# A spectral and windowed-attention mixer on one core: another layout of the spectra, and another order of early transfers

## The chip, the core and the metric

The program runs on one core of a Trainium2 chip. The metric is the device time of one execution in microseconds. TensorE is written PE, its weight loads PEld, VectorE DVE, ScalarE ACT, GpSimd POOL, and SyncE, which here only issues transfers, SP. ACT issues transfers too.

## The reference

The input is x, 2048 rows of 640 numbers in float32. Two branches are computed from it and mixed by a gate per row.

```python
g = _sigmoid((x * gate_w).sum(-1, keepdims=True))
a = _A_ref(x, A_wqkv, A_wo)      # q, k, v = x @ wqkv; 32 heads of 20; each row attends to 8 rows, 2 apart; @ wo
b = _B_ref(x, B_w_r, B_w_i)      # irfft2(rfft2(x) * (w_r + 1j * w_i))
return g * a + (1 - g) * b
```

## The kernel before

**Rows.** The 2048 rows are split as 128 partitions by 16 positions j (row = 16 p + j). A transform over rows is then a transform over the 128 partitions (a product with a table of cosines and sines) and one over the 16 positions.

**Recording and planning.** No instruction is issued where it is written. `Plan.record` (L224) notes every operation with what it must follow, `Plan.order` (L282) searches an order for each of the five engines with made-up costs, and `issue` (L472) then issues them in that order. That is why nearly all instructions of the profile carry the same line, L655: parts are told apart by the names of their tiles. An engine works through its list strictly in order, so an instruction that waits holds up everything behind it on that engine, transfers that it would issue included. `p.chain` and `p.rank` are hints for the search.

**Stages.** They overlap, and the PE list runs through them in this order:

1. `qkv` (L719): eight units (par, hg), each eight groups of 15 products of 480 columns. ACT copies a PSUM bank to `ev`, and for each pair ACT issues a store to `qkvd` in device memory. The weights of the next hg come by `load_w` (L673): SP loads `raw{hg}_{t}`, ACT makes a rounded copy and POOL the rest.
2. `attend` (L759): 16 halves of units, each a chain over DVE, POOL and ACT. Keys `kt` come by SP, queries `q` and values `vt` by ACT (L774 to L776), all from `qkvd`. ACT copies two positions of q at a time to `qbank`, DVE multiplies into `pr` and sums into the logits `L`. `mask` (L826) lets ACT write -1e9 to a few places of one partition of L. Units 0 and 4 come first.
3. `fold` and `cols` (L840, L878): x folded by symmetry, then products with the table `fc` into z; ACT copies z to `zg`, the spectra. `fold` of q = 2 and 3 stores its result to `fd` in device memory (L872) for later.
4. `freq` (L900): 16 groups g of frequencies, four staged at a time. A group takes its 8 columns (4 frequencies, real and imaginary) of the 16 positions: 128 numbers per chunk t. Weight of a product are these 128 columns, and the moving operand a table `bt`. This gives u and v, DVE makes ab = u + vv and u - vv, then come a transform over positions (xa, xc), the product with the filter (POOL, DVE: P, p, s), and the way back (g), which ACT copies to `zg`.
5. `project_even` (L1110), in between: rows j even of the attention output times wo (oTp, woa, wob).
6. `spatial` (L1025): for each position j, products whose weights are the 128 columns of `zg` at that j, and whose moving operand is the table `gt`: oa and ob, each one product of 322 columns and two of 161. Then ha and hb.
7. `project_odd` (L1126): rows j odd, to the end.

A float32 product is two passes on PE, each with its own weight load; the page counts passes, so oa has 16 x 3 x 2 = 96.

**What the change touches in `freq` and `spatial`.** `zg` lies as (chunk t, position j, 128 columns): the 128 columns at one t and j, the weights of `spatial`, are side by side. Those of a group are 16 runs of 8. So `freq` first copies them to `zc`, with the halves of the complex numbers exchanged in three further chunks for v:

```python
zc = self.zcr.next(f"zc{g}", 6, NJ, 8)
A.copy(zc[:, 0:3], zg[:, 0:3, :, 8 * g : 8 * g + 8])
A.mul(zc[:, 3:6, :, 0:4], zg[:, 2:5, :, 8 * g + 4 : 8 * g + 8], -1.0)
A.copy(zc[:, 3:6, :, 4:8], zg[:, 2:5, :, 8 * g : 8 * g + 4])
```

Of the kernel before, what the change touches and what calls it, by code (L numbers as in the profile page):

```python
# [17 lines left out]
NJ = 16  # L18
# [14 lines left out]
def dft_tables():  # L33
# [23 lines left out]
    bt = np.zeros((640, 642))  # L57
# [8 lines left out]
    j, k2 = np.arange(16), np.arange(16)  # L66
    md = np.zeros((16, 16, 2, 4, 2, 16, 4))
# [40 lines left out]
        first[x, x, 0] = g0  # L108
        first[x, x, 1, :, :, :, 0], first[x, x, 1, :, :, :, 1] = -g0[:, :, :, 1], g0[:, :, :, 0]
    first[:, :, :, :, :, 0, :, :, 0] = one  # L110
    first = first.reshape(8, 128, 128).transpose(1, 0, 2).reshape(128, 1024)
    mfu, mfv = mf[0].copy(), mf[0].copy()
    for q, w in ((mfu, mu), (mfv, mv)):
        q[:, :, 0] = 0
        q[:, :, 0, :, :, 0] = w
    first = np.concatenate([first, mfu.reshape(128, 128), mfv.reshape(128, 128)], 1)
    md = md.reshape(16, 128, 2, 64)
    mm = np.concatenate([-md[:, :, 1], md[:, :, 0], md[:, :, 1], mf.reshape(16, 128, 128)], 2)[1:]

    d = np.arange(161)  # L120
# [20 lines left out]


class Op:
    __slots__ = ("i", "eng", "name", "call", "busy", "lat", "size", "preds", "succs", "chain", "tail", "start", "end", "early", "group", "of", "two", "rank")


class Engine:
# [9 lines left out]
class Plan:  # L157
# [5 lines left out]
    def __init__(self, nc):  # L163
        self.ops, self.places, self.past = [], {}, set()
        self.chain = self.group = ""
        self.rank = 0.0
        self.code = {}
        for attr, eng, real in (
            ("pe", "PE", nc.tensor),
            ("dve", "DVE", nc.vector),  # L170
            ("act", "ACT", nc.scalar),
            ("pool", "POOL", nc.gpsimd),
            ("sp", "SP", nc.sync),
        ):
            setattr(self, attr, Engine(self, eng, real))
# [48 lines left out]
    def record(self, eng, name, fn, a, k):  # L224
        op = Op()
        op.i, op.eng, op.name, op.chain, op.group = len(self.ops), eng, name, self.chain, self.group
        op.preds, op.succs, op.size, op.early, op.two, op.rank = set(), [], 0, False, False, 0.0
        line = sys._getframe(2).f_lineno
        code = self.code.get(line)
        if code is None:  # L230
            code = self.code[line] = compile("\n" * (line - 1) + "fn(*a, **k)", __file__, "exec")
        op.call = (code, {"fn": fn, "a": a, "k": k})
        aps = [v for v in list(a) + list(k.values()) if hasattr(v, "tensor") and hasattr(v, "ap")]
        out = k["out"] if "out" in k else a[0]
        ins = [v for v in aps if v is not out]
        for v in ins:
            self.touch(op, v, False)
        self.touch(op, out, True)
        op.of = out.tensor.name
        self.cost(op, out, ins, k)  # L240
        self.ops.append(op)

    def cost(self, op, out, ins, k):
        n = max(int(np.prod(v.shape[1:])) for v in [out] + ins[:1])
        if op.name == "dma_start":
            op.busy, op.lat = {"SP": 0.45, "ACT": 0.45, "POOL": 1.0}[op.eng], LAND
            op.size = int(np.prod(out.shape)) * 4
            op.early = not hasattr(ins[0].tensor, "tag")
            if self.rank:
                op.rank, self.rank = self.rank, self.rank - 1e3  # L250
        elif op.eng == "PE":
            n = int(np.prod(out.shape[1:]))
            if op.name == "transpose":
                op.busy = 0.109
            elif ins[-1].dtype == F32R:
                op.busy = n / 2400 + 0.018
            else:
                op.busy = max(4 * n / 2400 + 0.006, 0.182)
            op.lat = 0.25
        elif op.eng == "DVE":  # L260
            op.busy, op.lat = 0.075 + n / 960, 0.12
            two = sum(v.tensor.tag[:4] not in ("bank", "qban") for v in ins) == 2
            if op.name == "scalar_tensor_tensor":
                op.busy += 0.06
            elif op.name == "reciprocal":
                op.busy += n * 0.007
            elif two:
                op.two = True
        elif op.eng == "ACT":
            strided = any(len(v.ap) > 2 and v.ap[-1][0] > 1 for v in [out] + ins)  # L270
            op.busy, op.lat = 0.12 + n * (1.75e-3 if strided else 0.78e-3), 0.15
            if len(ins) > 1:
                op.busy += 0.1
            if any(v.offset >= 64 * v.ap[0][0] for v in [out] + ins):
                op.busy += 0.08
        else:
            spread = any(v.ap[-1][0] == 0 for v in ins)
            op.busy, op.lat = 0.09 + n * (2e-3 if spread else 2.25e-3), 0.14
        if op.eng in ("DVE", "ACT", "POOL") and not op.size:
            op.busy *= PACE  # L280

    def order(self):  # L282
# [7 lines left out]
        for op in reversed(ops):  # L290
            op.tail = max([s.tail + self.lag(op, s) for s in op.succs], default=0.0)
            if op.size:
                op.tail += op.size / RATE
            key = (op.eng, op.chain)
            if key in last and (op.eng == "PE" or op.chain and op.eng != "ACT"):
                op.tail = max(op.tail, last[key].tail)
            op.tail += op.busy
            last[key] = op
        span = max(op.tail for op in ops)
        for op in ops:  # L300
            op.early = max(FOLD * (op.chain == "fold"), span - op.tail - AHEAD) if op.early and not op.rank else 0.0
# [211 lines left out]
class Mixer:  # L513
# [17 lines left out]
    def places(self, pp, dr, sb):  # L531
# [15 lines left out]
        def ring(*tags):  # L547
            return Ring(sb, *tags)

        def n(tag, k):  # L550
            return ring(*(f"{tag}{i}" for i in range(k)))
# [5 lines left out]
        self.xr, self.wr, self.evr, self.rawr, self.fr = n("x", 8), ring(*WPLACES), n("ev", 2), n("raw", 5), n("f", 2)  # L557
        self.er, self.xor = ring("fe0", "fe1"), ring("raw0", "raw1", "raw2", "raw3", "raw4", "kv4", "kv5", "ya")

        self.zcr, self.vsr, self.mdr, self.mfr, self.wpr = n("raw", 2), ring("raw2"), n("ev", 2), ring("mf"), n("f", 2)  # L560
        self.abr, self.Pr, self.s12r, self.Xr = ring("x0", "x1"), ring("x2", "x3"), ring("x4", "x5"), ring("raw3", "raw4")
        self.p1r = ring("x6")

        self.wor, self.war, self.yar = ring("ya", "w7"), ring("w2", "w3", "w4", "w0", "w1", "w5", "w6"), ring("ya")
        self.otr, self.oTr = (ring("w7"), ring("w7", "kv2")), (ring("x7"), ring("x7", "pr0"))
# [12 lines left out]
    def work(self):  # L578
# [26 lines left out]
        for hg in (1, 2, 3):  # L605
            self.load_w(None, hg)
            self.qkv(0, hg)
            if hg == 1:
                self.qkv(1, hg)
        self.zg = self.one("zg", 5, NJ, 128, tag="big")  # L610
        todo = list(range(8))

        def columns(jj):
# [59 lines left out]
    def load_w(self, st, hg):  # L673
# [4 lines left out]
        for t in range(5):  # L678
# [2 lines left out]
            hi.append(w[:, 0, 0:n])  # L681
            lo.append(w[:, 1, 0:n])
            if st is None:
                p.sp.dma_start(raw, src[t])
            p.chain = "w" if st is None else ""
            p.act.copy(hi[t], raw)
            (p.dve if st is not None else p.pool).tensor_sub(lo[t], raw, hi[t].bitcast(F32))
# [71 lines left out]
    def attend(self, par, h, step=4):  # L759
# [11 lines left out]
        p.chain = "logits"  # L771
        kt, vt = (self.kvr.next(f"{i}t{nm}", 15, HC) for i in "kv")
        q = self.qr.next(f"q{nm}", 8, HC)
        self.queue("kt").dma_start(kt.rearrange("p a b -> p (a b)"), rows(1, 0, 15), max_dma_last_dim=PACKET)  # L774
        self.queue("q").dma_start(q.rearrange("p a b -> p (a b)"), rows(0, 7, 8), max_dma_last_dim=PACKET)
        self.queue("vt").dma_start(vt.rearrange("p a b -> p (a b)"), rows(2, 0, 15), max_dma_last_dim=PACKET)  # L776
        L = self.Lr.next(f"L{nm}", 8, 4, 8)
        for jj in range(0, 8, 2):
            pr = self.prr.next(f"pr{nm}{jj}", 2, 8, HC)
# [60 lines left out]
    def fold(self, q):  # L840
# [28 lines left out]
        V.tensor_sub(f[:, :, 161:321], e[:, :, 0:160], eh[:, :, 160:0:-1])  # L869
        self.folded[q] = f  # L870
        if q in STORED:
            p.act.dma_start(self.f_d[:, q], f)  # L872

    def load_f(self, q):
        f = self.folded[q] = self.fr.next(f"f{q}", 2, 641)[:, :, 0:640]
# [2 lines left out]
    def cols(self, q):  # L878
        p = self.p
        f = self.folded[q]  # L880
        for t0, n in ((0, 2), (2, 2), (4, 1)):
            z = self.ps(BQ, f"z{q}_{t0}")
            for i in range(2 * n):
# [8 lines left out]
                )  # L892
            p.chain = "z"
            p.act.copy(
                self.zg[:, t0 : t0 + n, 2 * q : 2 * q + 2, :].rearrange("p t j c -> p t (j c)"),
                z[:, 0 : 256 * n].rearrange("p (t m) -> p t m", t=n),
            )
            p.chain = ""

    def freq(self, g):  # L900
# [12 lines left out]
        wp = self.wpr.next(f"wp{g}", 4, 321)  # L913
        self.queue("wp").dma_start(wp, ins["ws"][g])

        zc = self.zcr.next(f"zc{g}", 6, NJ, 8)
        A.copy(zc[:, 0:3], zg[:, 0:3, :, 8 * g : 8 * g + 8])
        A.mul(zc[:, 3:6, :, 0:4], zg[:, 2:5, :, 8 * g + 4 : 8 * g + 8], -1.0)
        A.copy(zc[:, 3:6, :, 4:8], zg[:, 2:5, :, 8 * g : 8 * g + 4])

        def row(o, t, r, start, stop):
            T.matmul(o, zc[:, t].rearrange("p j c -> p (j c)"), r, start=start, stop=stop, skip_group_check=True)

        v = self.ps(BV, f"v{g}")[:, 0:321]
        row(v, 4, bt[:, 803:1124], True, False)
        row(v[:, 0:161], 3, bt[:, 642:803], False, False)
        row(v[:, 161:321], 5, bt[:, 1124:1284], False, True)
        vv = self.vsr.next(f"vs{g}", 321)
        A.copy(vv, v)
        u = self.ps(BU, f"u{g}")[:, 0:321]  # L930
        row(u, 1, bt[:, 161:482], True, False)
        row(u[:, 0:161], 0, bt[:, 0:161], False, False)
# [7 lines left out]
        def col(nm, i, turned):  # L940
# [7 lines left out]
                c = 0 if turned else 64  # L948
                T.matmul(o, tb[:, c : c + 128], ab[:, i], start=True, stop=True)
            return o  # L950

        def turn(to, o):

            A.mul(to[0:64], o[64:128], -1.0)
            A.copy(to[64:128], o[0:64])

        X = self.Xr.next(f"X{g}", 2, 321)
        o = col("xa", 0, 0)
# [32 lines left out]
        for t0, n in ((0, 3), (3, 2)):  # L991
            o = self.ps(BG, f"g{g}_{t0}")
            for i in range(n):
# [8 lines left out]
                        skip_group_check=True,  # L1002
                    )
            A.copy(
                zg[:, t0 : t0 + n, :, 8 * g : 8 * g + 8],
                o[:, 0 : n * 128].rearrange("p (t j c) -> p t j c", t=n, c=8),
            )

    def load_wo(self):
# [15 lines left out]
    def spatial(self, j):  # L1025
# [3 lines left out]
        o1, o2 = (self.ps((0, 1, 2), f"o{i}{j}") for i in "ab")  # L1029

        def mm(o, t, r, start, stop):
            T.matmul(o, zg[:, t, j], r, start=start, stop=stop, skip_group_check=True)

        mm(o1[:, 0:322], 1, gt[:, 161:483], True, False)
        mm(o1[:, 0:161], 0, gt[:, 0:161], False, False)
# [201 lines left out]
```

## Time and profile before

| | |
|---|---|
| time, median of 3 runs | 453.15 us (453.03 to 455.2) |
| the profiled execution's own time | 452.6 us |
| its span | 450.8 us |
| PE busy | 443.1 us, 2437 products |
| DVE busy | 393.0 us |
| POOL busy | 339.3 us |
| ACT busy | 217.8 us, 578 instructions |
| transfers | 98.65 MB, 219 GB/s on average |
| granted PE clock | 1.00 |

Instruction spans on PE overlap: a product's span is longer than its distance to the next. The distance is read from the chain of work that ended last, where consecutive pieces are laid end to end, or from the start of the next row. "Idle before" is the time in which an engine had nothing running, with what ended it.

### The profile page before, as it was taken

How to read it: one execution, taken by the hardware profiler on the slowest of the kernel's cores; microseconds unless marked ns; L12 is line 12 of the kernel's file. 1: busy time of each engine (PE TensorE's matmuls, PEld its weight loads, DVE VectorE, ACT ScalarE, POOL GpSimd, SP SyncE). 2: the span in 40 equal slices, each digit the busy share in tenths (PEclk: the TensorE clock that was granted, in tenths of full speed). 3: DMA queues.
4: the chain of work that ended last, by engine and by line, in shares of the span. 5: the costliest groups of instructions: out<-in, count | busy, mean ns of one | idle time of the engine just before them, and what ended most of it. 6: DMA issues, size and time to landing. Idle time of an engine off the chain costs nothing. (4 is left out here: it accounts for less than half of the span.)

```text
span 450.8 us, 7124 instructions
## 1 busy us (share of the span) xinstructions
PE 443.1 (98%) x2437; PEld 388.8 (86%) x2437; DVE 393.0 (87%) x515; ACT 217.8 (48%) x578; POOL 339.3 (75%) x296
## 2 busy tenths in 40 slices
PE   9999999999999999999999999999999999999996
PEld 5888888888888889888987887899888999999996
DVE  5465699999999999999999999999999999989442
ACT  6464264324332333444558787878664654342120
POOL 1085047789999998899559899936498977967895
PEclk9999999999999999999999999999999999999999
DMA  8998949685665839999798676867634231769842
GB/s 313 371 316 283 354 148 313 209 273 138 210 195 160 247 115 284 300 288 288 230 268 294 177 246 191 282 222 239 197 120 129 86 98 52 190 170 230 295 147 87
DMA packets 87283, 98.65 MB, mean 219 GB/s; under 512 B 20416, under 2 KB 74816, under 8 KB 87248
## 3 DMA queue, kind: packets, MB, share of 16 engines
q1 hardware_dynamic: 47616, 63.64, 44.6%
q10 hardware_dynamic: 38864, 32.86, 23.7%
q0 software_dynamic: 768, 1.71, 2.1%
q8 instruction: 19, 0.31, 0.3%
q14 instruction: 16, 0.13, 0.1%
HBM read 66.33 MB, written 30.22 MB: 214 GB/s over the span
## 5 line engine op out<-in xcount | busy, mean ns | idle before, releaser
L655 PE MATMUL qkv<-w,xo 128*128 128x480 f32 (+1 forms) x480 | 114.2, 386 | 0.0
L655 PE MATMUL qkv<-w,xe 128*128 128x480 f32 (+1 forms) x465 | 105.3, 383 | 0.0
L655 PEld LDWEIGHTS qkv<-w,xo 128*128 128x128 f32 x480 | 89.2, 189 | 13.3 <-ACT ev L655 0.2
L655 PEld LDWEIGHTS qkv<-w,xe 128*128 128x128 f32 x465 | 87.4, 188 | 15.1 <-POOL w L655 0.5
L655 ACT COPY ev<-qkv 128x480 f32<-128x480 f32 x64 | 35.6, 558 | 46.6 <-PE qkv L655 29.6
L655 PE MATMUL woa<-wo,oT 128*128 128x320 f32 x240 | 47.7, 315 | 0.3 <-ACT oT L655 0.3
L655 PE MATMUL wob<-wo,oT 128*128 128x320 f32 x240 | 47.9, 317 | 0.0
L655 PEld LDWEIGHTS woa<-wo,oT 128*128 128x128 f32 x240 | 38.0, 188 | 0.8 <-ACT oT L655 0.6
L655 PEld LDWEIGHTS wob<-wo,oT 128*128 128x128 f32 x240 | 38.1, 188 | 0.4
L655 POOL TENSOR_TENSOR P<-X,wp 128x642 f32<-128x642 f32 x16 | 25.1, 1566 | 14.9 <-ACT X L655 14.7
L655 POOL TENSOR_TENSOR w<-raw,w 128x480 fp32r<-128x480 f32 x15 | 18.0, 1239 | 19.8 <-ACT w L655 19.8
L655 POOL TENSOR_TENSOR xo<-xt,xo 128x640 fp32r<-128x640 f32 x8 | 12.4, 1573 | 21.9 <-ACT xo L655 21.9
L655 ACT CAST oT<-oTp 128x384 fp32r<-128x384 f32 (+1 forms) x32 | 13.2, 428 | 28.6 <-PE woa L655 12.0
L655 PEld LDWEIGHTS g<-mm,s 128*128 128x128 f32 x150 | 21.9, 191 | 5.3 <-issue 0.7
L655 PE MATMUL g<-mm,s 128*128 128x128 f32 x150 | 23.5, 276 | 1.0 <-DVE s L655 0.8
L655 DVE TENSOR_TENSOR oT<-oTp,oT 128x384 fp32r<-128x384 f32 (+1 forms) x32 | 15.1, 484 | 8.9 <-ACT oT L655 8.9
L655 PE MATMUL oa<-gt,zg 128*128 128x161 f32 (+1 forms) x96 | 22.8, 344 | 0.0
L655 PE MATMUL ob<-gt,zg 128*128 128x161 f32 (+1 forms) x96 | 22.7, 345 | 0.0
L655 PE MATMUL v<-bt,zc 128*128 128x321 f32 (+2 forms) x96 | 22.2, 345 | 0.4 <-ACT zc L655 0.4
L655 PE MATMUL u<-bt,zc 128*128 128x321 f32 (+2 forms) x96 | 22.1, 344 | 0.0
L655 PEld LDWEIGHTS u<-bt,zc 128*128 128x128 f32 x96 | 15.8, 190 | 2.9
L655 PEld LDWEIGHTS v<-bt,zc 128*128 128x128 f32 x96 | 15.6, 190 | 3.0 <-ACT zc L655 0.6
(305 smaller groups left out, 1091.4 us busy)
## 6 DMA issues: line engine op xcount, KB each, us to landing
qkvd<-ev ACTq DMA_DIRECT2D x32, 480.0 KB, 4.1
wp<-in_ws SPq DMA_DIRECT2D x16, 642.0 KB, 4.6
fx<-in_x SPq DMA_DIRECT2D x8, 648.0 KB, 7.3
ot<-od SPq DMA_DIRECT2D x16, 320.0 KB, 3.8
raw<-in_wqkv SPq DMA_DIRECT2D x15, 240.0 KB, 5.0
xt<-in_xT SPq DMA_DIRECT2D x8, 320.0 KB, 8.6
ad<-ya SPq DMA_DIRECT2D x8, 320.0 KB, 2.5
yi<-ad SPq DMA_DIRECT2D x8, 320.0 KB, 3.8
```

Source lines behind the costliest of these rows:

```text
L655: p.dve.memset(w, 0.0)
```

## The change

`zg` now lies as (t, group g, the 8 columns c of the group, position j). The 128 numbers of a group at one t are side by side and are the weights of u and v directly; `zc` is gone. The tables are permuted to fit (columns outside, positions inside). The exchange of the halves for v is made on v itself, when ACT copies it from PSUM: two copies of 64 partitions (`turn`) for one of 128. The copy of z to `zg` now writes numbers 16 apart (64 bytes), and the copy of g to `zg` writes whole runs. In `spatial` the 128 weights of a position are 16 numbers, or 64 bytes, apart. The place of `zc` goes to a second buffer of `vs` and of p.

Second, a flag `hold` on some transfers: in the plan they follow the first key and query loads (unit 0, half a). They are the weights of hg = 2, the keys and queries of half b of unit 0, the values of half a, and the stores of `fold`. The planner is told so; no wait is added on the chip by it, only the lists change.

```diff
@@ dft_tables
-    first = first.reshape(8, 128, 128).transpose(1, 0, 2).reshape(128, 1024)
+    first = first.transpose(0, 1, 2, 4, 5, 3, 6, 7, 8).reshape(8, 128, 128).transpose(1, 0, 2).reshape(128, 1024)
...
-    md = md.reshape(16, 128, 2, 64)
+    md = md.transpose(0, 2, 3, 1, 4, 5, 6).reshape(16, 128, 2, 64)
+    mf = mf.transpose(0, 1, 2, 3, 5, 6, 4)
@@ Plan.order
+        for op in ops:
+            if op.hold:
+                op.preds.update(self.keys)
+                for k in self.keys:
+                    k.succs.append(op)
+                    k.tail = max(k.tail, op.tail)
@@ Mixer.places
-        self.zcr, self.vsr, self.mdr, self.mfr, self.wpr = n("raw", 2), ring("raw2"), n("ev", 2), ring("mf"), n("f", 2)
+        self.vsr, self.mdr, self.mfr, self.wpr = n("raw", 2), n("ev", 2), ring("mf"), n("f", 2)
...
-        self.p1r = ring("x6")
+        self.p1r = ring("x6", "raw2")
@@ Mixer.work
-        self.zg = self.one("zg", 5, NJ, 128, tag="big")
+        self.zg = self.one("zg", 5, 16, 8, NJ, tag="big")
@@ Mixer.load_w
+                p.hold = hg == 2
                 p.sp.dma_start(raw, src[t])
+                p.hold = False
@@ Mixer.attend
+        p.hold = f and u == 0
         self.queue("kt").dma_start(kt.rearrange("p a b -> p (a b)"), rows(1, 0, 15), max_dma_last_dim=PACKET)
         self.queue("q").dma_start(q.rearrange("p a b -> p (a b)"), rows(0, 7, 8), max_dma_last_dim=PACKET)
+        if (par, h) == (0, 0):
+            p.keys, p.hold = p.ops[-2:], True
         self.queue("vt").dma_start(vt.rearrange("p a b -> p (a b)"), rows(2, 0, 15), max_dma_last_dim=PACKET)
+        p.hold = False
@@ Mixer.cols
-                self.zg[:, t0 : t0 + n, 2 * q : 2 * q + 2, :].rearrange("p t j c -> p t (j c)"),
-                z[:, 0 : 256 * n].rearrange("p (t m) -> p t m", t=n),
+                self.zg[:, t0 : t0 + n, :, :, 2 * q : 2 * q + 2].rearrange("p t g c j -> p t j (g c)"),
+                z[:, 0 : 256 * n].rearrange("p (t j c) -> p t j c", t=n, j=2),
@@ Mixer.freq
-        zc = self.zcr.next(f"zc{g}", 6, NJ, 8)
-        A.copy(zc[:, 0:3], zg[:, 0:3, :, 8 * g : 8 * g + 8])
-        A.mul(zc[:, 3:6, :, 0:4], zg[:, 2:5, :, 8 * g + 4 : 8 * g + 8], -1.0)
-        A.copy(zc[:, 3:6, :, 4:8], zg[:, 2:5, :, 8 * g : 8 * g + 4])
+        def turn(to, o):
+
+            A.mul(to[0:64], o[64:128], -1.0)
+            A.copy(to[64:128], o[0:64])
...
-            T.matmul(o, zc[:, t].rearrange("p j c -> p (j c)"), r, start=start, stop=stop, skip_group_check=True)
+            T.matmul(o, zg[:, t, g].rearrange("p c j -> p (c j)"), r, start=start, stop=stop, skip_group_check=True)
...
-        A.copy(vv, v)
+        turn(vv, v)
...
-                zg[:, t0 : t0 + n, :, 8 * g : 8 * g + 8],
-                o[:, 0 : n * 128].rearrange("p (t j c) -> p t j c", t=n, c=8),
+                zg[:, t0 : t0 + n, g].rearrange("p t c j -> p t (c j)"),
+                o[:, 0 : n * 128].rearrange("p (t m) -> p t m", t=n),
@@ Mixer.spatial
-            T.matmul(o, zg[:, t, j], r, start=start, stop=stop, skip_group_check=True)
+            T.matmul(o, zg[:, t, :, :, j].rearrange("p g c -> p (g c)"), r, start=start, stop=stop, skip_group_check=True)
```

Three places show how the lists change. The first is SP's list where the first keys are asked for; `raw2_t` are the weights of hg = 2, `kt0a` and `kt0b` the keys of unit 0. Before:

```order
L655 DMA fc_70<-in_t_fc 128x128
L655 DMA raw2_0_192<-in_wqkv 128x480
L655 DMA raw2_1_194<-in_wqkv 128x480
L655 DMA raw2_2_196<-in_wqkv 128x480
L655 DMA kt0a_321<-qkvd_64 128x4x300
L655 DMA kt0b_337<-qkvd_64 128x4x300
L655 DMA raw2_3_198<-in_wqkv 128x480
```

And of the changed kernel:

```order
L666 DMA fc_70<-in_t_fc 128x128
L666 DMA kt0a_321<-qkvd_64 128x4x300
L666 DMA kt0b_337<-qkvd_64 128x4x300
L666 DMA raw2_0_192<-in_wqkv 128x480
L666 DMA raw2_1_194<-in_wqkv 128x480
L666 DMA raw2_2_196<-in_wqkv 128x480
L666 DMA raw2_3_198<-in_wqkv 128x480
```

Three loads of weights moved from ahead of the keys to behind them. The second place is ACT's list at the same time; `fd` are the stores of `fold`, `q0a`, `q0b`, `vt0a` and `vt0b` loads of unit 0, `ev` copies of PE's results, `qbank` the copies that the first products of DVE read. Before:

```order
L655 DMA fd_67<-fx2_136 128x2x640
L655 COPY ev4_0_147<-qkv4_0_146 128x6x80
L655 COPY z_72<-qkv4_0_146 128x1
L655 DMA q0a_323<-qkvd_64 128x2x320
L655 DMA q0b_339<-qkvd_64 128x2x320
L655 DMA vt0a_322<-qkvd_64 128x4x300
L655 DMA fd_67<-fx3_141 128x2x640
L655 DMA vt0b_338<-qkvd_64 128x4x300
L655 COPY ev4_0_147<-qkv4_1_148 128x6x80
```

And of the changed kernel:

```order
L666 COPY ev4_0_147<-qkv4_0_146 128x6x80
L666 COPY z_72<-qkv4_0_146 128x1
L666 DMA q0a_323<-qkvd_64 128x2x320
L666 COPY ev4_0_147<-qkv4_1_148 128x6x80
L666 COPY z_72<-qkv4_1_148 128x1
L666 DMA qkvd_64<-ev4_0_147 128x6x160
L666 COPY ev4_2_150<-qkv4_2_149 128x6x80
L666 COPY qbank_63<-q0a_323 128x160 x3
L666 COPY z_72<-qkv4_2_149 128x1
L666 DMA q0b_339<-qkvd_64 128x2x320
L666 DMA fd_67<-fx2_136 128x2x640
L666 DMA vt0a_322<-qkvd_64 128x4x300
```

Five transfers moved behind the first copies to `qbank`, and the copies of PE's results moved ahead of them. The third place is ACT's list where `freq` begins, behind the last copies of z. Before:

```order
L655 COPY zg_236<-z7_4_306 128x256
L655 COPY zg_236<-z7_2_305 128x2x256
L655 ACTIVATE zc1_583<-zg_236 128x48x4
L655 COPY zc1_583<-zg_236 128x48x4
L655 COPY zg_236<-z7_0_304 128x2x256
L655 COPY zc1_583<-zg_236 128x384
L655 ACTIVATE zc2_592<-zg_236 128x48x4
L655 COPY zc2_592<-zg_236 128x48x4
L655 COPY vs1_585<-v1_584 128x321
```

And of the changed kernel:

```order
L666 COPY zg_236<-z7_2_305 128x2x2x128
L666 COPY zg_236<-z7_4_306 128x2x128
L666 COPY zg_236<-z7_0_304 128x2x2x128
L666 ACTIVATE vs1_584<-v1_583 64x321
L666 COPY vs1_584<-v1_583 64x321
```

The copies to `zc` are gone, and the copy of v is two.

More of the change, by code (lines that the diff above doesn't have):

```diff
@@ L115, in dft_tables @@
         q[:, :, 0, :, :, 0] = w
-    first = np.concatenate([first, mfu.reshape(128, 128), mfv.reshape(128, 128)], 1)
-    md = md.reshape(16, 128, 2, 64)
+    mfu, mfv = (q.transpose(0, 1, 2, 4, 5, 3).reshape(128, 128) for q in (mfu, mfv))
+    first = np.concatenate([first, mfu, mfv], 1)
+    md = md.transpose(0, 2, 3, 1, 4, 5, 6).reshape(16, 128, 2, 64)
+    mf = mf.transpose(0, 1, 2, 3, 5, 6, 4)
     mm = np.concatenate([-md[:, :, 1], md[:, :, 0], md[:, :, 1], mf.reshape(16, 128, 128)], 2)[1:]
@@ L143 @@
 class Op:
-    __slots__ = ("i", "eng", "name", "call", "busy", "lat", "size", "preds", "succs", "chain", "tail", "start", "end", "early", "group", "of", "two", "rank")
+    __slots__ = ("i", "eng", "name", "call", "busy", "lat", "size", "preds", "succs", "chain", "tail", "start", "end", "early", "group", "of", "two", "rank", "hold")
 class Engine:
@@ L165, in __init__ @@
         self.chain = self.group = ""
-        self.rank = 0.0
+        self.rank, self.hold, self.keys = 0.0, False, []
         self.code = {}
@@ L227, in record @@
         op.preds, op.succs, op.size, op.early, op.two, op.rank = set(), [], 0, False, False, 0.0
+        op.hold = False
         line = sys._getframe(2).f_lineno
@@ L248, in cost @@
             op.early = not hasattr(ins[0].tensor, "tag")
+            op.hold = self.hold
             if self.rank:
@@ L871, in fold @@
         if q in STORED:
+            p.hold = True
             p.act.dma_start(self.f_d[:, q], f)
+            p.hold = False
     def load_f(self, q):
@@ L914, in freq @@
         self.queue("wp").dma_start(wp, ins["ws"][g])
-        zc = self.zcr.next(f"zc{g}", 6, NJ, 8)
-        A.copy(zc[:, 0:3], zg[:, 0:3, :, 8 * g : 8 * g + 8])
-        A.mul(zc[:, 3:6, :, 0:4], zg[:, 2:5, :, 8 * g + 4 : 8 * g + 8], -1.0)
-        A.copy(zc[:, 3:6, :, 4:8], zg[:, 2:5, :, 8 * g : 8 * g + 4])
+        def turn(to, o):
+            A.mul(to[0:64], o[64:128], -1.0)
+            A.copy(to[64:128], o[0:64])
         def row(o, t, r, start, stop):
-            T.matmul(o, zc[:, t].rearrange("p j c -> p (j c)"), r, start=start, stop=stop, skip_group_check=True)
+            T.matmul(o, zg[:, t, g].rearrange("p c j -> p (c j)"), r, start=start, stop=stop, skip_group_check=True)
         v = self.ps(BV, f"v{g}")[:, 0:321]
-        row(v, 4, bt[:, 803:1124], True, False)
-        row(v[:, 0:161], 3, bt[:, 642:803], False, False)
-        row(v[:, 161:321], 5, bt[:, 1124:1284], False, True)
+        row(v, 3, bt[:, 803:1124], True, False)
+        row(v[:, 0:161], 2, bt[:, 642:803], False, False)
+        row(v[:, 161:321], 4, bt[:, 1124:1284], False, True)
         vv = self.vsr.next(f"vs{g}", 321)
-        A.copy(vv, v)
+        turn(vv, v)
         u = self.ps(BU, f"u{g}")[:, 0:321]
@@ L950, in col @@
             return o
-        def turn(to, o):
-            A.mul(to[0:64], o[64:128], -1.0)
-            A.copy(to[64:128], o[0:64])
         X = self.Xr.next(f"X{g}", 2, 321)
```

## Prediction

> **What bounds the kernel now.** I read the busy times by stage first: the last copies of the qkv stage with z, then `freq`, `spatial`, and the odd rows. Columns: stretch, its length, then busy time (and instructions) of PE, PEld, DVE, ACT, POOL, the granted clock, the share and rate of transfers.
>
> ```profile
> 170.00:235.00 65.00, 64.92 (x375) 58.08 (x373) 63.51 (x77) 28.30 (x72) 51.40 (x42) 1.00 0.92 280
> 235.00:338.00 103.00, 101.08 (x604) 86.46 (x604) 98.21 (x163) 80.44 (x225) 79.58 (x69) 1.00 0.69 217
> 338.00:405.00 67.00, 66.76 (x420) 61.08 (x420) 63.66 (x84) 33.51 (x87) 57.13 (x48) 1.00 0.43 122
> 405.00:447.00 42.00, 41.19 (x289) 40.46 (x288) 24.07 (x47) 6.75 (x17) 34.38 (x46) 1.00 0.64 196
> ```
>
> PE has no room anywhere: idle are 1.92 us in `freq` (103.00 - 101.08), 0.24 in `spatial`, 0.81 in the odd rows, 0.08 in the stage of z, together 3.05 us. DVE is nearly as full up to 405 us. ACT is full nowhere. So ACT work that goes away is worth nothing by itself, a microsecond added to PE's stream is worth a microsecond, and the most that any relief elsewhere can bring is about 3 us. The waits of PE say who causes the idle part (total, times, longest):
>
> ```profile
> PE g L655 <- DVE s L655: 0.8, 2, 0.5
> PE xc L655 <- DVE s L655: 0.5, 1, 0.5
> PE oTp L655 <- DMA ot<-od: 0.5, 1, 0.5
> PE v L655 <- ACT zc L655: 0.4, 1, 0.4
> ```
>
> Mostly DVE being late; the copies to `zc` account for 0.4 us, once. For the change, the question is then what it does to DVE's start and to PE's own pace.
>
> **Part 1: the loads of keys.** These rows show SP's list and ACT's with start and length, DVE's first use of the keys and POOL's of the values, a wait of POOL, then the time from issue to landing of the first keys and of an undisturbed load of the same size:
>
> ```profile
> 38.09 2.80 SPq L655 DMA_DIRECT2D raw<-in_wqkv  x3
> 40.98 0.47 SPq L655 DMA_DIRECT2D kt0a<-qkvd  x1
> ...
> 36.73 0.37 ACTq L655 DMA_DIRECT2D qkvd<-ev  x1
> 37.52 0.37 ACTq L655 DMA_DIRECT2D fd<-fx  x1
> 40.60 0.37 ACTq L655 DMA_DIRECT2D q0a<-qkvd  x1
> ...
> 59.11 21.15 PE L655 MATMUL qkv<-w,xe 128*128 128x480 f32 x95
> ...
> 38.33 0.55 ACT L655 COPY ev<-qkv 128x480 f32<-128x480 f32 x1
> 49.10 1.49 DVE L655 TENSOR_TENSOR pr0a<-kt0a,qbank 128x1280 f32<-128x1280 f32 x1 [7.90 <-DMA kt0a<-qkvd]
> 74.95 1.50 POOL L655 TENSOR_TENSOR pv0a<-vt0a,L0a 128x640 f32<-128x640 f32 x1
> POOL w L655 <- ACT w L655: 19.8, 1, 19.8
> ...
> kt0a<-qkvd SPq DMA_DIRECT2D x1, 600.0 KB, 8.0
> kt5a<-qkvd SPq DMA_DIRECT2D x1, 600.0 KB, 3.6
> ```
>
> The keys can't be asked for before the last store of unit 0 (issued at 36.73) has landed; the queries, which wait for the same, go at 40.60. So the earlier place in SP's list brings only 40.98 - 40.60 = 0.4 us. The rest of the gain is the landing: 8.0 us with three weight loads and a store of `fold` (0.72 and 0.64 MB) in front, 3.6 us at best. That is up to 4.4 + 0.4 = 4.8 us. But in the changed list of ACT the first copies to `qbank` stand behind the copy of the third product of unit 4. Copies of successive products come 3.3 us apart (15 products of 0.22 us, since 95 take 21.15); the first of unit 4 ran at 38.3, so the third can't before about 45, and DVE starts at 46 instead of 49.1. I take 3 us, between 0 (landing as slow as now) and 4.8. What moved behind (queries of half b, values, weights of hg = 2) is needed later: DVE first has about 12 us of half a (four products and four sums of 1.49), values are first used at 74.9, and POOL idles 19.8 us before the weights. A 3 us head start of DVE can remove DVE's part of PE's idle time. I take 2.5 us of the 3.05, with 0 and 3.1 as ends.
>
> **Part 2: ACT in `freq`.** Per group three copies go, and one becomes two; the last two rows, the copies of z, get a step of 64 bytes:
>
> ```profile
> L655 ACT COPY zc<-zg 128x384 f32<-128x384 f32 x16 | 8.1, 512 | 0.1
> L655 ACT ACTIVATE zc<-zg 128x192 f32<-128x192 f32 x16 | 5.9, 366 | 0.0
> L655 ACT COPY zc<-zg 128x192 f32<-128x192 f32 x16 | 5.5, 346 | 0.0
> L655 ACT COPY vs<-v 128x321 f32<-128x321 f32 x16 | 6.8, 426 | 0.5 <-PE v L655 0.5
> L655 ACT ACTIVATE X<-xa 64x321 f32<-64x321 f32 x15 | 6.5, 436 | 2.8 <-PE xa L655 2.4
> L655 ACT COPY X<-xa 64x321 f32<-64x321 f32 x15 | 6.3, 419 | 0.2
> L655 ACT COPY zg<-z 128x512 f32<-128x512 f32 x16 | 9.2, 588 | 10.4 <-PE z L655 10.3
> L655 ACT COPY zg<-z 128x256 f32<-128x256 f32 x8 | 3.0, 380 | 1.2 <-PE z L655 1.2
> ```
>
> The removed busy time is 8.1 + 5.9 + 5.5 = 19.5 us. The new `turn` is the same pair as that of X: 16 x (436 + 419 - 426) = 6.9 us more. Net 12.6 us less ACT work, in a stage where ACT is busy 80.4 of 103 us: worth the 0.4 us of PE's wait and no more (it is among the 3.05).
>
> **Part 3: what a step of 64 bytes costs.** No PE row of this trace reads with a step. ACT has a few that write with one. In `mask`, 16 numbers go in pairs (the first two rows) or singly with 32 bytes between them (the third, the last of the four copies); the group rows give the price of more numbers side by side:
>
> ```profile
> 52.20 0.20 ACT L655 COPY L0a<-low 1x16 f32<-1x16 f32 x1 [1.28 <-DVE L0a L655]
> 55.26 0.20 ACT L655 COPY L0a<-low 1x16 f32<-1x16 f32 x1 [1.23 <-DVE L0a L655]
> 61.29 0.22 ACT L655 COPY L0a<-low 1x16 f32<-1x16 f32 x1 [0.61 <-DVE L0a L655]
> ...
> L655 ACT COPY zg<-g 128x384 f32<-128x384 f32 x16 | 7.7, 478 | 2.7 <-PE g L655 2.6
> L655 ACT COPY zg<-g 128x256 f32<-128x256 f32 x16 | 6.0, 374 | 2.4 <-PE g L655 2.3
> ```
>
> Side by side a number costs (478 - 374) / 128 = 0.81 ns; alone about 0.02 us / 16 = 1.2 ns more (0.6 to 1.9, as the rows have two decimals). I estimate 1.75 ns per lone number, double. For the copies of z, 16 of 512 and 8 of 256 numbers, that is 10240 x 0.94 ns = 9.6 us more on ACT, beside PE and DVE work in a stage where ACT is busy 28.3 of 65 us: hidden. At the start of `freq` u waits for the last z, now about 0.5 us later; v no longer waits for `zc` (0.4 us). I set these off.
>
> PE's loads in `spatial` are another matter.
>
> ```profile
> L655 PEld LDWEIGHTS oa<-gt,zg x96: 186/190/192, 338.5 to 402.7; 128*128 128x128 f32 x96
> L655 PE MATMUL oa<-gt,zg x96: 297/300/455, 338.6 to 402.9; 128*128 128x161 f32 x64, 128*128 128x322 f32 x32
> ...
> 347.19 1.09 PE ob L655 x6
> ...
> 279.03 0.67 PE g L655 x6
> ```
>
> Six passes of ob take 1.09 us: two of 322 columns and four of 161, which at one pace per column are 0.27 and 0.137 us. In g (128 columns) passes follow at 0.67 / 6 = 0.111 us, so a load with its numbers side by side is no hindrance at 111 ns. A load starts only about 0.1 us ahead of its pass (338.5 and 338.6), so I assume one load per pass, under way during the pass before. If a lone number costs PE what it costs ACT, a load takes 128 x 1.75 = 224 ns.
>
> Per o (32 of them) two of six loads hide under a pass of 322 columns, four stand against passes of 0.137 us: 32 x 4 x (224 - 137) = **11.1 us** on PE. The ends: nothing if a load stays under 137 ns; at 300 ns, all six late, 128 x 163 + 64 x 30 = 22.8 us. I take 11.1, since the ACT rows are the only ones with a step. The stage has 0.24 us idle on PE, nothing hides it.
>
> The Trainium skill ("SBUF — State Buffer", Specifications) has SBUF in lines of 16 bytes and asks for two or more hits per line for full bandwidth. The pairs and lone numbers of `mask` agree with it, at 0.02 us; it names no price for a load, so by it the loads only become slower.
>
> **Sum**, against the profiled execution's 452.6 us (0.5 us below the median of 453.15): 452.6 - 2.5 + 11.1 = 461.2, so **461 us**.
>
> **Rivals.** (a) Loads with a step cost nothing extra, or stay below the 137 ns of a pass. For it: the loads of this trace take 186 to 192 ns each whatever they read, and yet pass every 111 ns, so they are long in latency and not in pace. Against it: the ACT rows. Then only part 1 is left: 452.6 - 2.5 = 450.1 us, and the point from which it decides is 137 ns. The Trainium skill ("TensorE: Matmul & The Clock Gate", LDWEIGHTS) has a load take its columns / 1.2 ns whatever the rest; by that rule the time is this rival's, and the 111 ns in g agree with its 107. (b) A load with a step costs far more, 300 ns: 452.6 - 2.5 + 22.8 = 472.9 us. For it: a float32 load comes twice per product and may fetch its numbers in parts; against it: nothing here is that slow per number. (c) A price in between, 140 to 165 ns: 128 x 3 to 28 = 0.4 to 3.6 us, so 450.5 to 453.7. (d) The keys don't land earlier, because the store ahead of them is the limit, or DVE's lead is used up before `freq`: with the price of part 3, 463.7 us.
>
> **How the numbers follow.** Forecast 0.45 (456 to 464), (a) 0.32 (449.3 to 452.6), (b) 0.10, (c) 0.07, (d) 0.06. The range reaches over (a), (c) and (d) to 449.5 and 465, leaving out (b) and the margins. Half a percent of 453.15, about what a measurement of this kernel can tell from no change, is 2.3 us: faster means below 450.9, slower above 455.4. Slower is the forecast, (b) and (d): 0.61. Of (a) I put 0.19 below 450.9; its remaining 0.13 with (c) makes 0.20 for the same.
>
> **What would show it.** In the changed profile, the rows of oa and ob: six passes in 1.43 us instead of 1.09 (2 x 0.27 + 4 x 0.224), and loads longer than 190 ns; if they are still 1.09 us, part 3 is wrong and (a) holds. DVE's first pr0a near 46 us instead of 49.1, with a wait of about 5 us instead of 7.9, else part 1 is wrong. PE idle below 1 us in `freq`. Copies of 512 numbers of z near 1.07 us instead of 0.59, and no new wait of PE for them; a wait of PE for `zg` there would be a cost that I put at nothing.

## The result, and the profile after

| | before | after |
|---|---|---|
| time, median of 4 runs each, taken together | 453.91 us (453.03 to 455.2) | 465.84 us (464.31 to 466.49) |
| ratio | | 1.0247, 95% interval 1.0224 to 1.027 |
| profiled execution, its span | 452.6 us, 450.8 us | 464.31 us, 462.5 us |

The change makes the kernel slower by 2.5%. First come the busy times of the whole span in the profile after, and its windows of the stages (columns as in the prediction):

```profile
PE 454.7 (98%) x2437; PEld 404.6 (87%) x2437; DVE 394.9 (85%) x515; ACT 221.2 (48%) x546; POOL 339.9 (73%) x296
```

```profile
170.00:235.00 65.00, 65.00 (x377) 58.46 (x376) 63.42 (x75) 35.46 (x70) 54.25 (x44) 1.00 0.89 272
235.00:338.00 103.00, 101.62 (x600) 85.94 (x599) 97.25 (x161) 75.96 (x194) 78.52 (x67) 1.00 0.70 217
338.00:405.00 67.00, 66.43 (x365) 65.52 (x364) 58.48 (x70) 29.54 (x77) 50.75 (x43) 1.00 0.36 101
```

PE runs the same 2437 passes and is idle as long as before: 462.5 - 454.7 = 7.8 us, against 450.8 - 443.1 = 7.7. So the time is not in a wait for another engine. PE is busy longer, with the same work, and the third window says where: from 338 to 405 us it gets through 365 passes instead of 420, while busy for 66.43 of the 67 us. The loads and the chain of work there show why:

```profile
L666 PEld LDWEIGHTS oa<-gt,zg x96: 291/310/320, 339.6 to 415.1; 128*128 128x128 f32 x96
L666 PEld LDWEIGHTS ob<-gt,zg x96: 291/310/315, 342.3 to 416.5; 128*128 128x128 f32 x96
```

```profile
342.63 1.41 PE ob L666 x6
...
345.74 1.42 PE ob L666 x6
```

A load takes 310 ns instead of 190, and six passes of ob 1.41 us instead of 1.09. If the two loads that run under passes of 322 columns (0.27 us each) cost nothing, the other four passes take (1.41 - 0.54) / 4 = 217 ns each; 224 was forecast. The same rows of the loads in the kernel before, with first and last start, are:

```profile
L655 PEld LDWEIGHTS oa<-gt,zg x96: 186/190/192, 338.5 to 402.7; 128*128 128x128 f32 x96
L655 PEld LDWEIGHTS ob<-gt,zg x96: 186/190/192, 340.0 to 404.1; 128*128 128x128 f32 x96
```

From the first load of oa to the last of ob it is now 416.5 - 339.6 = 76.9 us, against 404.1 - 338.5 = 65.6 before: 11.3 us more. The records of the passes of ob, before and after, show where it lies:

```profile
L655 PE MATMUL ob<-gt,zg x96: 297/300/503, 340.0 to 404.2; 128*128 128x161 f32 x64, 128*128 128x322 f32 x32
L666 PE MATMUL ob<-gt,zg x96: 300/382/542, 342.5 to 416.7; 128*128 128x161 f32 x64, 128*128 128x322 f32 x32
```

Taken one by one, of the 192 passes of oa and ob in the kernel after, all 140 that follow a shorter pass last longer than before, by 82 ns on average, and none of the 52 that follow a pass of 322 columns does. So a pass waits where its load had too little time under the pass ahead of it: 140 x 82 ns = 11.5 us.

### The profile page after: what moved, and what is told of

It is laid out like the page before. It is cut to its first block, busy times and chain, and to the rows that moved or that the text cites. A ratio compares the mean times of both kernels' runs of the same rounds, so it can differ in the third digit from the quotient of the medians.

```text
span 462.5 us, 7087 instructions
## 1 busy us (share of the span) xinstructions
PE 454.7 (98%) x2437; PEld 404.6 (87%) x2437; DVE 394.9 (85%) x515; ACT 221.2 (48%) x546; POOL 339.9 (73%) x296
## 4 chain that ended last, share of the span: by engine, by line
PE 78%; issue 7%; DVE 5%; DMA 5%; POOL 3%; ACT 2%; ACTq 0%; POOLq 0%; DVEq 0%
PE qkv L666 33%; PE woa L666 7%; PE wob L666 6%; PE oa L666 5%; PE ob L666 5%; PE z L666 4%; PE v L666 3%; PE g L666 3%; PE u L666 3%; PE hb L666 2%; PE ha L666 2%; DMA xt<-in_xT 2%; PE oTp L666 2%; POOL xo L666 2%; PE xa L666 2%
## 5 line engine op out<-in xcount | busy, mean ns | idle before, releaser
L666 PE MATMUL woa<-wo,oT 128*128 128x320 f32 x240 | 49.2, 316 | 0.1
L666 PE MATMUL oa<-gt,zg 128*128 128x161 f32 (+1 forms) x96 | 28.0, 408 | 0.6 <-ACT zg L666 0.6
L666 PE MATMUL ob<-gt,zg 128*128 128x161 f32 (+1 forms) x96 | 26.6, 402 | 0.0
L666 PEld LDWEIGHTS g<-mm,s 128*128 128x128 f32 x150 | 20.9, 191 | 4.3 <-ACT zg L666 2.0
L666 PEld LDWEIGHTS oa<-gt,zg 128*128 128x128 f32 x96 | 23.8, 305 | 0.8 <-ACT zg L666 0.8
L666 PEld LDWEIGHTS ob<-gt,zg 128*128 128x128 f32 x96 | 24.1, 305 | 0.0
L666 ACT COPY zg<-z 128x512 f32<-128x512 f32 (+1 forms) x24 | 20.7, 948 | 6.4 <-PE z L666 6.4
L666 PE MATMUL u<-bt,zg 128*128 128x321 f32 (+2 forms) x96 | 22.4, 345 | 0.0
```

The source lines that it names most:

```text
L666: p.dve.memset(w, 0.0)
```

## The experiments

In some of these kernels the operand of an instruction is replaced after the order has been planned. The five lists are then word for word those of the kernel that it starts from, and only what the instruction reads differs.

**Only the step, in the kernel before.** The weights of oa and ob are read with a step of 16 numbers; nothing else differs. The products then take other numbers of `zg` than the reference's.

```diff
             T.matmul(o, zg[:, t, j], r, start=start, stop=stop, skip_group_check=True)
+            call = p.ops[-1].call[1]
+            w = zg[:, t].rearrange("p j c -> p (j c)").rearrange("p (i s) -> p s i", s=16)[:, j]
+            call["a"] = (o, w, r)
```

> The kernel before, with its lists of instructions unchanged; only the weights of oa and ob are read with 64 bytes between the numbers (so other numbers are taken, and the second branch comes out as another result). Theory S (the step of the loads is the loss): loads of 310 ns as in the changed kernel, six passes of oa or ob in about 1.41 us instead of 1.09, about 11 us more than before: 464 to 467 us. Rival L (the loads are only longer in latency and the loss is in the changed lists, the copies of z and the wait at the start of spatial): 453 to 455 us.

Measured: 466.35 us (464.83 to 467.49) beside 453.87, ratio 1.0266 (1.024 to 1.0293). The loads by tile:

```profile
L655 PEld LDWEIGHTS oa<-gt,zg x96: 291/310/319, 340.3 to 415.6; 128*128 128x128 f32 x96
L655 PEld LDWEIGHTS ob<-gt,zg x96: 291/310/317, 342.2 to 417.3; 128*128 128x128 f32 x96
```

The 310 ns and the stretch (77.0 us) are those of the changed kernel, and so is the time, within the intervals. The step alone makes a loss as large as the whole change does.

**All but the step, in the kernel after.** The reverse: the lists and everything else of the changed kernel, with the weights of oa and ob read side by side. Again the products take other numbers of `zg`.

```diff
             T.matmul(o, zg[:, t, :, :, j].rearrange("p g c -> p (g c)"), r, start=start, stop=stop, skip_group_check=True)
+            call = p.ops[-1].call[1]
+            call["a"] = (o, zg[:, t, j].rearrange("p c j -> p (c j)"), r)
```

> The changed kernel with its lists unchanged; only the weights of oa and ob are read side by side (128 neighbours of the same store, so other numbers, and the second branch comes out as another result). Theory S: six passes in 1.09 us again, the time falls by 11 us to 453 to 456 us, and what it stands above or below the kernel before (453.9) is all that the rest of the change does. Rival L: 464 to 466 us as the changed kernel.

Measured: 454.59 us, ratio to before 1.0011 (0.9996 to 1.0027). All loads of oa are back at 190 ns:

```profile
L666 PEld LDWEIGHTS oa<-gt,zg x96: 187/190/192, 339.4 to 404.9; 128*128 128x128 f32 x96
```

So the earlier keys and the 32 fewer copies on ACT are together worth nothing that can be measured, where the prediction counted a gain of 2.5 us: the interval reaches from 0.2 us faster to 1.2 us slower. The next four kernels ask why.

**Only the hold.** The kernel before, with the flag `hold` alone: the hunks of `Plan.order`, `load_w` and `attend`, and the one of `fold` that sets the flag for its stores. Two places of it:

```diff
+            if op.hold:
+                op.preds.update(self.keys)
...
+        if (par, h) == (0, 0):
+            p.keys, p.hold = p.ops[-2:], True
```

> The kernel before with the second part of the change alone (the transfers planned behind the first keys and queries). Theory D (DVE's early start is lost again within a few products, since the copies to qbank wait behind other work on ACT): 453 to 455 us, no change. Rival G (the early start is worth its 2.5 us, and only the other layout's lists gave it away): 451 to 452 us.

Measured: 455.24 us, ratio 1.0027 (1.0009 to 1.0044): a trace slower, not faster, and 0.2 us above the range of Theory D. DVE's first product, PE's busy time in `freq` and the first of PE's waits there are:

```profile
L664 DVE TENSOR_TENSOR pr0a<-kt0a,qbank x4: 1486/1486/1489, 46.2 to 56.1; 128x1280 f32<-128x1280 f32 x4
```

```profile
235.00:338.00 103.00, 100.04 (x589) 84.12 (x590) 98.45 (x161) 79.48 (x223) 81.95 (x69) 1.00 0.67 215
```

```profile
PE xa L664 <- DVE ab L664: 1.5, 2, 0.8
PE g L664 <- DVE s L664: 0.4, 1, 0.4
PE xc L664 <- DVE s L664: 0.4, 1, 0.4
```

DVE starts at 46.2, just as forecast, 2.9 us earlier than before. Yet PE is idle in `freq` for 103.00 - 100.04 = 2.96 us instead of 1.92. The head start came, and PE got nothing from it; but the lists were planned anew here, and differ elsewhere too.

**Only the layout.** The kernel after without the hold.

```diff
-            if op.hold:
+            if False and op.hold:
```

> The changed kernel with the first part alone (layout and exchange at v's copy; no transfer is held back). Theory D with S: 464.5 to 467 us, the same as the changed kernel within 0.3%. Rival G: about 2.5 us above the changed kernel, 468 us. A third case: the held transfers cost something, then 463 us or less.

Measured: 467.59 us, ratio 1.0299 (1.0279 to 1.0319), 1.8 us above the median of the changed kernel. By the time alone that is nearer to Rival G's 468 than to Theory D, whose range it leaves; where PE is idle has to decide. Two of PE's waits, from the list for the whole program, then DVE's first product and the window of `freq`. In the kernel after, the first wait is absent and the second is 0.2 us:

```profile
PE qkv L666 <- ACT ev L666: 1.1, 1, 1.1
...
PE qkv L666 <- POOL w L666: 0.6, 1, 0.6
...
51.64 1.49 DVE L666 TENSOR_TENSOR pr0a<-kt0a,qbank 128x1280 f32<-128x1280 f32 x1 [9.98 <-ACT qbank L666]
...
235.00:338.00 103.00, 102.03 (x609) 87.03 (x608) 98.26 (x158) 76.39 (x195) 80.50 (x69) 1.00 0.70 224
```

In the lists that the planner makes for the new layout without the hold, PE waits 1.1 us for a copy to `ev`; with the hold it does not. DVE starts 3.8 us later than in the kernel after, and still PE is idle in `freq` for 0.97 us instead of 1.38. So the 1.8 us don't come from DVE's start in the way that the prediction meant: most of them are PE's waits for ACT and POOL in the first 100 us. Why these are late there was not tried.

**A lead for DVE by itself, early.** To take the planner out of the question: the kernel before, its lists as they were, with the eight sums of unit 0 adding one number in place of 20 (its logits are then other ones). A sum takes 0.28 us instead of 1.49 (the 0.15 us expected below was too low), so that DVE has 9.6 us less to do there.

```diff
+            if (par, h) in ((0, 0), (0, 1)):
+                call = p.ops[-1].call[1]
+                call["k"] = dict(call["k"], in_=pr.rearrange("p j r (h d) -> p j r h d", d=HD)[:, :, :, :, 0:1])
```

> The kernel before with its lists unchanged; the sums of the first two halves of unit 0 (8 instructions of DVE) add one number instead of 20 and so take about 0.15 us instead of 1.49, which leaves out part of these two heads' logits. DVE gains some 10 us of lead by 75 us. Theory D (what PE waits for in freq is the chain of a few instructions and not DVE's total): at most 1 us faster, 452.9 to 454.5 us. Rival G (a lead of 3 us or more takes 2.5 us of PE's waits away): 451.4 us or less.

Measured: 454.04 us beside 454.1, ratio 1.0004 (0.9982 to 1.0025): a gain of 2.5 us is excluded. Three of DVE's waits from 45 to 110 us, and ACT's timeline at the longest of the new ones:

```profile
DVE pr0a L655 <- ACT qbank L655: 3.3, 1, 3.3
DVE m0b L655 <- ACT L0b L655: 3.0, 1, 3.0
DVE pr4a L655 <- ACT qbank L655: 2.6, 1, 2.6
```

```profile
51.33 0.65 ACTq L655 DMA_DIRECT2D qkvd<-ev  x1
...
57.86 0.56 ACT L655 COPY ev<-qkv 128x480 f32<-128x480 f32 x1 [3.96 <-DMA qkvd<-ev]
58.32 0.30 ACT L655 COPY qbank<-q0b 128x160 f32<-128x160 f32 x1
```

Of those three only the last stands in the kernel before, with 0.6 us. So 8.3 of the 9.6 us are gone by 75 us. At the longest wait DVE's next product needs a copy to `qbank`. That copy stands in ACT's list behind a copy to `ev`, and this one waits until the store of 51.33 has landed and its buffer is free. ACT's list sets the pace of DVE here, and a faster DVE only waits.

**The same lead, late.** Perhaps a lead is worth something if it is still there when `freq` begins. The same edit for the unit whose logits are L3a and L3b, from 193 to 242 us.

```diff
-            if (par, h) in ((0, 0), (0, 1)):
+            if (par, h) in ((0, 6), (0, 7)):
```

> The kernel before, with every list as it was; only the eight sums of half a and half b of the unit whose logits are L3a and L3b (193 to 242 us) add one number in place of 20 and take about 0.28 us in place of 1.48, so that DVE has 9.6 us less to do just before and at the start of freq (the logits of that unit are then not the reference's). It asks whether a lead that DVE has when freq begins is worth what the prediction gave to one at the start. Theory H (a lead there reaches PE): PE's waits for s in freq (0.8 and 0.5 us) go, PE is idle in 235 to 338 us about 1 us or less instead of 1.92, time 451.5 to 452.8 us beside 453.9. Theory N (DVE waits there too for what ACT, POOL or PE bring later in their own lists, so the lead is gone within 30 us): DVE's busy time in 170 to 235 falls by some 7 us with no change in PE's idle time in freq beyond 0.4 us, time 453.5 to 454.3 us.

Measured: 453.92 us beside 454.85, ratio 0.9984 (0.9959 to 1.0008). No gain is shown; the interval excludes 2.5 us, but not one below 2 us. The trace says more. PE's waits, and its idle time from 235 to 338 us, are those of before to the last digit or nearly (103.00 - 101.00 = 2.00 us, before 1.92), while DVE does 5.4 us less in that window (and 3.5 less in the stage before it, where Theory N expected 7):

```profile
235.00:338.00 103.00, 101.00 (x606) 86.51 (x606) 92.77 (x161) 80.77 (x225) 78.41 (x67) 1.00 0.68 218
```

```profile
PE g L655 <- DVE s L655: 0.8, 2, 0.5
PE xc L655 <- DVE s L655: 0.5, 1, 0.5
```

The timelines of PE, ACT and DVE of this kernel, around the first of these waits, tell why:

```profile
241.39 0.70 PE L655 MATMUL xc<-ab,mm 128*128 128x321 f32 x2
...
242.19 0.41 ACT L655 ACTIVATE xd<-xc 64x321 f32<-64x321 f32 x1 [0.44 <-PE xc L655]
...
242.63 0.49 DVE L655 TENSOR_TENSOR p<-xc,wp 128x321 f32<-128x321 f32 x1 [3.06 <-ACT xd L655]
243.04 0.88 DVE L655 TENSOR_TENSOR ab<-u,vs 128x321 f32<-128x321 f32 x2
243.84 0.49 DVE L655 TENSOR_TENSOR xd<-xd,wp 128x321 f32<-128x321 f32 x1
244.37 0.50 DVE L655 TENSOR_TENSOR xd<-p,xd 128x321 f32<-128x321 f32 x1
244.97 0.89 DVE L655 TENSOR_TENSOR s<-P,xd 128x321 f32<-128x321 f32 x2
...
245.51 0.71 PE L655 MATMUL g<-mm,s 128*128 128x128 f32 x4 [0.25 <-DVE s L655]
```

DVE is not late: it has been idle for 3.06 us when p starts. The wait is the time of a round that PE itself began: xc, ACT's copy, five steps of DVE (with two ab of another group between them, 0.80 us), back to g. It takes 245.51 - 241.39 = 4.1 us, and PE's list has a quarter of a microsecond too little other work to put into it. In the kernel before the same g waits the same 0.25 us, at 245.24. No lead of DVE shortens such a round. Another order within it, with ab behind s, was not tried; it would delay the products that read ab.

**What a step costs.** In the kernel before, two positions j each are read with a step of 1, 2, 3, 4, 6, 8, 12 and 16 numbers (4 to 64 bytes), with tiles named by the step. The weights are other numbers of `zg` than the reference's.

```diff
+        form = ("one", "two", "three", "four", "six", "eight", "twelve", "sixteen")[j // 2]
...
+            w = bass.AP(tensor=flat.tensor, offset=flat.offset, ap=[flat.ap[0], [step, 128]])
+            p.ops[-1].call[1]["a"] = (o, w, r)
```

> The kernel before with its lists unchanged; the weights of oa and ob are read with 1, 2, 3, 4, 6, 8, 12 or 16 numbers from one to the next, two positions j for each (other numbers are taken, so the second branch comes out as another result). Theory P (a load pays when its next number lies in another piece of 16 bytes): 190 ns at 1, little at 2 and 3, the full 310 ns from 4 on, the same at 4 as at 16. Rival Q (the price grows with the distance): 4 clearly below 16. Rival W (any step above 1 costs the whole): 310 ns at 2 already.

Measured: 462.74 us in one run. The loads of oa, by step (minimum, median and maximum in ns):

```profile
L655 PEld LDWEIGHTS oa_one<-gt,zg x12: 187/190/205, 341.8 to 380.4; 128*128 128x128 f32 x12
L655 PEld LDWEIGHTS oa_two<-gt,zg x12: 194/196/198, 339.1 to 384.2; 128*128 128x128 f32 x12
L655 PEld LDWEIGHTS oa_three<-gt,zg x12: 252/252/263, 342.6 to 388.8; 128*128 128x128 f32 x12
L655 PEld LDWEIGHTS oa_four<-gt,zg x12: 307/330/332, 352.6 to 393.9; 128*128 128x128 f32 x12
L655 PEld LDWEIGHTS oa_six<-gt,zg x12: 296/298/319, 357.7 to 401.6; 128*128 128x128 f32 x12
L655 PEld LDWEIGHTS oa_eight<-gt,zg x12: 312/334/337, 362.3 to 403.4; 128*128 128x128 f32 x12
L655 PEld LDWEIGHTS oa_twelve<-gt,zg x12: 341/367/372, 363.9 to 408.9; 128*128 128x128 f32 x12
L655 PEld LDWEIGHTS oa_sixteen<-gt,zg x12: 292/312/324, 366.9 to 412.3; 128*128 128x128 f32 x12
```

A step of 2 is nearly free, one of 3 costs 62 ns, and from 4 on it is 108 to 177 ns more, without an order by distance. So Theory P holds only in the main: a step of 3, which it counted as nearly free, has a price, and the loads from 4 on aren't alike. The rivals Q and W do not hold. The Trainium skill ("SBUF — State Buffer", Specifications) asks for two or more hits on a line of 16 bytes. A step of 2 numbers still has two in a line, one of 4 has one, and the rows agree; the page gives no price, and why 12 costs more than 16 these runs don't show. The Trainium skill's rule for a load, its columns / 1.2 ns ("TensorE: Matmul & The Clock Gate", LDWEIGHTS), has no term for the step. By it every load here would take 128 / 1.2 = 107 ns, an estimate; no record of a load is that short, and the records grow clearly from a step of 3 on.

**Gathering first.** If loads must be side by side, ACT can gather them: the kernel after, with one copy of 5 x 128 numbers per position ahead of its products.

```diff
+        zs = self.zsr.next(f"zs{j}", 5, 128)
+        A.copy(zs, zg[:, :, :, :, j].rearrange("p t g c -> p t (g c)"))
...
-            T.matmul(o, zg[:, t, :, :, j].rearrange("p g c -> p (g c)"), r, start=start, stop=stop, skip_group_check=True)
+            T.matmul(o, zs[:, t], r, start=start, stop=stop, skip_group_check=True)
```

> The changed kernel, and ACT copies the 640 spectra of a position side by side before oa and ob read them (16 copies of about 1.3 us each, the read with the step now on ACT). Theory S: loads of 190 ns, six passes in 1.09 us, and ACT, busy 30 of 67 us in spatial, hides its 21 us: 453.5 to 456 us. Rival: the copies stand in the way of os and h on ACT, and PE waits for them: 457 to 462 us.

Measured: 456.48 us, ratio to before 1.0049 (1.0031 to 1.0068), between the two forecasts. The group of the gathering copies, the window of `spatial`, and PE's longest wait there:

```profile
L667 ACT COPY zs<-zg 128x640 f32<-128x640 f32 x16 | 21.2, 1333 | 0.4 <-PE oa L667 0.4
```

```profile
338.00:405.00 67.00, 64.92 (x406) 58.75 (x405) 61.05 (x75) 50.38 (x98) 53.00 (x46) 1.00 0.41 115
```

```profile
PE ob L667 <- ACT zs L667: 1.1, 1, 1.1
```

The loads are at 190 ns again, and most of the loss is won back: ACT had room in `spatial`, and its 21.2 us are nearly all hidden. What remains is in part 67.00 - 64.92 = 2.08 us of idle time on PE in the window instead of 0.24. Of it 1.1 us are the first product of ob, which now follows a copy of 1.3 us; the others (0.7 of g, 0.3 of oTp) lie ahead of `spatial`, which starts later in this kernel. No version tried that computes the same result is faster than the kernel before.

## Why the prediction was right in its direction and low in its size

The median is 0.84 us above the top of the range. Against the profiled executions the forecast was 452.6 + 8.6; it became 452.6 + 11.7. The profiled executions lie 1.31 us below the median before and 1.53 below the median after. So without the gain of part 1 the sum, 463.7 us, comes within 0.6 us of the profiled 464.31.

- **The loads (+11.1 us): right in mechanism, and in size with some luck.** A pass every 217 ns instead of 224, 11.3 us more in the stretch, and by itself the step gave 466.35 - 453.87 = 12.5 us (1.024 to 1.0293, that is 10.9 to 13.3). The reading of "one load per pass, under way during the pass before" held: exactly the passes behind a short pass wait. The size was luck in part. The rows of `mask` allowed 0.81 + 0.6 to 0.81 + 1.9 ns a number, which is 180 to 347 ns a load. Summed in the same way that is 5.5 to 31.8 us, the upper end with all six loads late; 1.75 was a choice in the lower half. That ACT's price would be PE's was assumed; and the same loads at a step of 12 take 367 ns instead of 312. Also 140 passes wait, not 128, and 82 ns each, not 87.
- **Rivals (a), (b), (c): excluded.** (a) needed a pass of at most 137 ns, (c) 140 to 165, (b) 300; it is 217.
- **The step that failed: "A 3 us head start of DVE can remove DVE's part of PE's idle time. I take 2.5 us of the 3.05."** The start moved, by 2.9 us with the hold alone and by 1.2 us in the changed kernel. The first keys did land sooner, in the changed kernel 4.9 us after they were asked for instead of 8.0. DVE starts later there than with the hold alone, since ACT asks for the last store of unit 0 only at 38.95 us instead of 36.73:

```profile
38.95 0.37 ACTq L666 DMA_DIRECT2D qkvd<-ev  x1
...
47.88 1.49 DVE L666 TENSOR_TENSOR pr0a<-kt0a,qbank 128x1280 f32<-128x1280 f32 x1 [6.15 <-ACT qbank L666]
```

  But even the full 2.9 us bought nothing that shows, nor did 9.6 us, early or late. So the term is 0 in place of 2.5. Behind it stood one misread sentence, "Mostly DVE being late". PE's rows named s, the last link of a round that PE had started itself; and DVE, the engine named, had itself just waited for the copy of PE's xc. The row that shows it was in the trace of before, one view away, on DVE's own timeline:

```profile
242.36 0.49 DVE L655 TENSOR_TENSOR p<-xc,wp 128x321 f32<-128x321 f32 x1 [0.66 <-ACT xd L655]
```

  The other two waits of PE for DVE in `freq` (0.53 and 0.51 us) are alike: in their rounds DVE sat idle for 0.44 and 0.27 us before its p. No gain from the lead is what rival (d) had as its outcome, 463.7 us, at a chance of 0.06. A busy share of 98.21 / 103.00, which is 95%, is not yet a queue of late work.
- **A cost put at nothing: 0.6 us.** The first product of `spatial` waits for ACT's last copy to `zg`, as this row of PE's waits has it. The sum 452.6 + 11.1 + 0.6 gives 464.3, the profiled time; that it fits to the last digit is chance, as small terms of both signs are left out.

```profile
PE oa L666 <- ACT zg L666: 0.6, 1, 0.6
```

- **Part 2 and the copies of z: right.** Copies of 512 numbers were forecast at 1.07 us and took 1.09 on average (the row stands at the end), and no new wait of PE for them came in that stage. The work that ACT no longer does was worth no more than the 0.4 us of the wait for `zc`. PE's idle time in `freq` fell by 0.54 us, to 103.00 - 101.62 = 1.38, and not below 1.

## What to carry to other kernels

- A layout has two readers. Before it is turned for one of them, count how often the other reads with a step, and price that on the engine that has no room: here 140 loads that stand against short passes, at 82 ns each, outweighed everything that the copies had cost on an engine with time to spare.
- A wait names the last link of a chain. Before "engine X is late" is turned into microseconds, look at X's own timeline just ahead of it: if X was idle too, the wait is the length of a round, and only a shorter round or other work for the waiting engine removes it.
- A lead given to an engine lasts only until its next wait for an engine whose list is paced by something else; here 8.3 of 9.6 us were gone some 25 us after DVE's start.

## What the runs showed of the hardware

- The price of a step for a float32 load is not in order of distance: 196 ns at 8 bytes, 252 at 12, 330 at 16, and then 298, 334, 367 and 312 at 24, 32, 48 and 64 bytes. That 48 bytes cost more than 64 was not expected, and stays open.
- ACT pays about the same for reading with a step of 64 bytes as for writing with one. Writing 512 numbers (the copies of z) took 1092 ns on average instead of 588, which is (1092 - 588) / 512 = 0.98 ns more for each:

```profile
L666 ACT COPY zg<-z 128x512 f32<-128x512 f32 x16 | 17.0, 1092 | 6.4 <-PE z L666 6.4
```

  Reading 640 numbers (the gathering copies) took 1333 ns. In short runs they would take about 733, an estimate from the copies to `zc` in the prediction, which read `zg` in runs of 8 and 4: 512 ns for 384 numbers and 346 for 192, so 512 + 256 x 0.86. That is (1333 - 733) / 640 = 0.94 ns more for each.
